# Block transposes that write pairs at a step of 2 elements in place of runs at a step of 4, and loads in two transfers per piece

## The chip, the cores and the metric

The kernel runs on one core of one Trainium2 chip. The metric is the time of one execution on the device in microseconds (us). Engines: VectorE (DVE in the profile), TensorE (PE), ScalarE (ACT), SyncE (SP, which issues the loads here), and the DMA engines.

## The reference

A 1x1 grouped convolution in bf16: every pixel has 192 channels in 4 groups of 48, and each group is multiplied by its own 48x48 matrix.

```python
H = W = 512;  G = 4;  Cg = 48;  C = 192;  k = 1       # x: (1, 512, 512, 192) bf16, w: (1, 1, 4, 48, 48) bf16
xg  = x.reshape(B, H, W, G, Cg)
out = einsum('bhwgc,gcd->bhwgd', xg, w[0, 0]).reshape(B, H, W, C)
```

That is 262,144 pixels, 100.7 MB read and 100.7 MB written.

## The kernel before

Pixels lie on partitions when they are loaded, but the matmuls of this kernel contract over partitions, so the channels must get there. VectorE does this with 32x32 block transposes. One step takes 8 pixel columns (1024 pixels): per partition 4 pixel slots `u` with 384 contiguous elements each, 1536 in all. A transpose instruction (STREAM_TRANSPOSE in the profile) reads these runs in order and writes each 32-element row of a block into `xT`. A column of 128 elements in `xT` is then the stationary operand of a matmul, and the order of the elements in it is the order of the pixels in the matmul's output.

```python
NXT = 4; STEP = 8; NQ = 4; Q = 32; RCOLS = 512        # ring: 512 pixel columns, pieces of at most 128
# [... sizes, planning of pieces: 8, 8, 16, 32, 64, then 128s, then 64, 32, 16, 8, 8 columns ...]

@block.sync                                           # loads, one transfer per piece
def _(sp):
    for p in pieces:
        # [... wait for the stores of the pieces that held this part of the ring ...]
        src = pixels(xf, p).rearrange("(p i) c -> p (i c)", p=128)
        sp.dma_start(region(p), src).then_inc(ld_sem[p.i], 16)

@block.vector                                         # transposes, 256 of them
def _(dve):
    for s in range(NS):
        if s in first:
            wq.wait(ld_sem[first[s].i], 16)
        wq.wait(mm_done, s - NXT + 1)
        src = columns(s).rearrange("p u g (b j) -> p u (g b) j", j=Q)
        dst = xT[s % NXT][:].rearrange("p (b i u) -> p u b i", u=NQ, i=Q)   # i steps 4 elements = 8 bytes
        dve.transpose(dst, src).then_inc(t_done, 1)

# [... tensor: per step 12 matmuls of xT columns with block-diagonal weights, into PSUM ...]
# [... scalar: per step one copy PSUM -> ring, then the store of a finished piece: ...]
        dst = pixels(of, p).rearrange("(a q g) c -> q a (g c)", a=NQ, q=128)
        act.dma_start(dst, region(p).rearrange("p (a n) -> p a n", a=NQ)).then_inc(st_sem[p.i], 16)
```

## Time and profile before

| | before |
|---|---|
| time, median | 897.24 us (3 runs, 897.05 to 898.37) |
| VectorE busy | 874.9 us, 98% of the span of 895.0 us |
| VectorE busy per transpose | 874.9 / 256 = 3.418 us |
| ScalarE, TensorE busy | 371.2 us, 445.0 us |
| DMA | 27.2% + 27.0% of the 16 engines' span |

These are lines of the page of the kernel before: busy time of each engine, the chain of waits that ended last, and the costliest groups of instructions. A group's line gives busy us and the mean ns of one record, then the idle time before it and what ended that.

```profile
PE 445.0 (50%) x3072; PEld 290.0 (32%) x3072; DVE 874.9 (98%) x256; ACT 371.2 (41%) x261; POOL 1.9 (0%) x6
...
DVE 92%; issue 3%; ACTq 2%; PE 1%; DVEq 1%; ACT 0%; DMA 0%
...
L138 DVE STREAM_TRANSPOSE xT<-ring 128x1536 bf16<-128x1536 bf16 x256 | 874.9, 3635 | 14.0 <-PE o_ps L160 10.2
...
L190 ACT CAST ring<-o_ps 128x1536 bf16<-128x1536 f32 x256 | 367.9, 1438 | 510.7 <-PE o_ps L160 488.7
```

VectorE is the bound. One record is 3635 ns, but records of neighbours overlap by some 0.2 us; busy time divided by the count, 3.418 us, is what a step really takes. The timeline of ScalarE in the head of the kernel before (start, duration, engine and line, instructions, and in brackets the idle time before):

```profile
37.49 1.44 ACT L190 CAST ring<-o_ps 128x1536 bf16<-128x1536 f32 x1 [1.98 <-PE o_ps L160]
37.50 23.44 ACTq L184 DMA_DIRECT2D out_dram<-ring  x1
60.98 2.78 ACT L190 CAST ring<-o_ps 128x1536 bf16<-128x1536 f32 x2 [22.05 <-issue]
```

### The profile page before, as it was taken

The numbers are of one execution on the slowest core, as the hardware profiler recorded it, in microseconds if no ns is written. First come the engines' busy times: TensorE is split into PE (matmuls) and PEld (weight loads), VectorE is DVE, ScalarE is ACT, GpSimd is POOL, SyncE is SP. The second block draws the span as 40 slices with busy tenths as digits, with TensorE's granted clock in tenths as the row PEclk, the third lists the DMA queues.
The fourth block names the chain that finished last, engine by engine and source line by source line (L and its number), as shares of the span: only waits on it lengthen the run. The fifth ranks groups of instructions, "written<-read, shape, count | busy, mean of one in ns | idle before, by whom it ended". The sixth has DMA issues, their size and how long they took to land.

```text
span 895.0 us, 7034 instructions
## 1 busy us (share of the span) xinstructions
PE 445.0 (50%) x3072; PEld 290.0 (32%) x3072; DVE 874.9 (98%) x256; ACT 371.2 (41%) x261; POOL 1.9 (0%) x6
## 2 busy tenths in 40 slices
PE   3626766587666544444444434444444444444443
PEld 2314434344443323222232323232232323232222
DVE  8959999999999999999999999999999999999997
ACT  3315344434344344444434344444444343444443
POOL 0000000000000000000000000000000000000000
PEclk9658576755667899999999999999999999999999
DMA  9996419266390844809457192662917633060444
GB/s 385 427 413 252 211 71 388 106 282 282 141 385 38 351 212 192 362 10 389 174 236 327 53 396 114 282 282 97 396 70 299 264 149 133 1 281 1 192 186 185
DMA packets 16413, 201.79 MB, mean 225 GB/s; under 512 B 1024, under 2 KB 4096, under 8 KB 6912
## 3 DMA queue, kind: packets, MB, share of 16 engines
q1 hardware_dynamic: 3456, 100.66, 27.2%
q10 hardware_dynamic: 12928, 100.68, 27.0%
q8 instruction: 25, 0.41, 0.2%
q14 instruction: 4, 0.03, 0.0%
HBM read 100.68 MB, written 100.66 MB: 225 GB/s over the span
## 4 chain that ended last, share of the span: by engine, by line
DVE 92%; issue 3%; ACTq 2%; PE 1%; DVEq 1%; ACT 0%; DMA 0%
DVE xT L138 92%; ACTq L184 2%; PE o_ps L160 1%; DVEq L90 1%; ACT ring L190 0%; DMA ring<-in_x_dram 0%
## 5 line engine op out<-in xcount | busy, mean ns | idle before, releaser
L138 DVE STREAM_TRANSPOSE xT<-ring 128x1536 bf16<-128x1536 bf16 x256 | 874.9, 3635 | 14.0 <-PE o_ps L160 10.2
L160 PE MATMUL o_ps<-wt,xT 128*128 128x192 bf16 (+1 forms) x3072 | 445.0, 303 | 445.4 <-DVE xT L138 412.2
L190 ACT CAST ring<-o_ps 128x1536 bf16<-128x1536 f32 x256 | 367.9, 1438 | 510.7 <-PE o_ps L160 488.7
L160 PEld LDWEIGHTS o_ps<-wt,xT 128*128 128x128 bf16 x3072 | 290.0, 107 | 600.2 <-DVE xT L138 474.8
L176 ACT ACT_TABLE_LOAD x1 | 1.3, 1283 | 9.8 <-DMA w_sb<-in_w_dram 9.8
L176 ACT COPY wt<-w_sb 32x384 bf16<-32x384 bf16 x4 | 2.0, 510 | 0.1
L117 POOL MEMSET wt<- 128x1536 bf16 x1 | 1.4, 1372 | 0.0
L116 POOL MEMSET w_sb<- 32x384 bf16 x1 | 0.4, 407 | 0.3 <-POOLq L212 0.3
L212 POOL MEMSET const-bfloat16-1.0<- 128x1 bf16 x1 | 0.1, 102 | 0.0
L212 POOL MEMSET const-uint8-127<- 128x1 uint8 x1 | 0.1, 102 | 0.0
L212 POOL MEMSET const-float32-0.0<- 128x1 f32 x1 | 0.1, 99 | 0.2 <-issue 0.2
L212 POOL MEMSET const-float32-1.0<- 128x1 f32 x1 | 0.1, 99 | 0.0
## 6 DMA issues: line engine op xcount, KB each, us to landing
ring<-in_x_dram SPq DMA_DIRECT2D x14, 6144.0 KB, 18.0
out_dram<-ring ACTq DMA_DIRECT2D x14, 6144.0 KB, 16.5
ring<-in_x_dram SPq DMA_DIRECT2D x2, 3072.0 KB, 13.5
out_dram<-ring ACTq DMA_DIRECT2D x2, 3072.0 KB, 9.9
ring<-in_x_dram SPq DMA_DIRECT2D x2, 1536.0 KB, 11.8
out_dram<-ring ACTq DMA_DIRECT2D x2, 1536.0 KB, 19.7
ring<-in_x_dram SPq DMA_DIRECT2D x4, 384.0 KB, 9.8
ring<-in_x_dram SPq DMA_DIRECT2D x2, 768.0 KB, 10.9
```

The source lines that it names most:

```text
L90: with ExitStack() as es:
L116: gp.memset(w_sb[:], 0.0).then_inc(wz_sem, 1)
L117: gp.memset(wt[:], 0.0).then_inc(tz_sem, 1)
L138: dve.transpose(dst, src).then_inc(t_done, 1)
L160: ins = pe.matmul(o, lhsT=xs[:, at:at + 128], rhs=r, start=(b == 1), stop=(b == 2), skip_group_check=True)
L176: act.copy(dst, w_sb[:]).then_inc(wc_sem, 1)
L184: act.dma_start(dst, src).then_inc(st_sem[p.i], 16)
L190: act.copy(dst, src).then_inc(o_done, 1)
L212: nc = _bacc.Bacc("TRN2", target_bir_lowering=False, num_devices=1)
```

## The change

The intent: let consecutive writes of a transpose land close together, in pairs of neighbouring 4-byte words, while the loads keep packets half as long as before. Writes of one run go to elements 0, 2, then 8, 10, then 16, 18 and so on, in place of 0, 4, 8, 12. To make the pixel order come out right, a piece is loaded as two transfers, each with a packet of 24,576 bytes per partition for the large pieces, not 49,152.

```diff
-                src = pixels(xf, p).rearrange("(p i) c -> p (i c)", p=128)
-                sp.dma_start(region(p), src).then_inc(ld_sem[p.i], 16)
+                src = pixels(xf, p).rearrange("(r u b n) c -> u r b (n c)", r=64, u=2, b=2)
+                half = p.size * C // 2
+                for u in range(2):
+                    sp.dma_start(region(p)[:, u * half:(u + 1) * half], src[u]).then_inc(ld_sem[p.i], 16)
 ...
-                    wq.wait(ld_sem[first[s].i], 16)
+                    wq.wait(ld_sem[first[s].i], 32)
                 wq.wait(mm_done, s - NXT + 1)
-                src = columns(s).rearrange("p u g (b j) -> p u (g b) j", j=Q)
-                dst = xT[s % NXT][:].rearrange("p (b i u) -> p u b i", u=NQ, i=Q)
+                src = columns(s).rearrange("p (w v) g n -> p w v (g n)", w=2, v=2)
+                dst = xT[s % NXT][:].rearrange("p (b w i v) -> p w v b i", w=2, i=2, v=2)
                 dve.transpose(dst, src).then_inc(t_done, 1)
```

## The prediction

Passages that say of the hardware what no trace or run of this case shows are cut from the prediction and from the expectations, and the cuts are marked. In the prediction the two terms of the step are a cost per element and a fixed cost per instruction, neither taken from a trace; their sum was a pitch of 1.69 to 1.82 us. The sums that follow rest on it: 433 to 466 us over 256 steps, 239 x 1.7 to 1.8 us on the VectorE path and, coupled with DMA, the forecast of 508 us.

> **What bounds the kernel now.** VectorE. The page's first part has it busy 874.9 of 895.0 us (98%), and the chain of waits is 92% the block transpose. In the stage-by-stage chain sixteen transposes (one 128-column piece) take 54.66 us, so the pitch is 3.416 us, for 1536 elements per partition: 2.22 ns an element. 256 x 3.416 = 874.5 us. Everything else has room: ScalarE's eviction 1.44 us a step (368 us in all); TensorE's 12 matmuls 1.48 us a step at full clock (2.74 us at the low clock of the first 300 us); DMA busy 27.2 + 27.0% of the span, 487 us.
>
> **Why the transpose costs 2.2 ns.** Source runs are contiguous; writes step 4 elements (8 bytes)[...].[...]
>
> **What the change does.** Same instruction count on VectorE, TensorE, ScalarE. Write order becomes element 0, 2, then 8, 10, then 16, 18: pairs in adjacent words[...]. Expected: [...]1.69 to 1.82 us pitch[...], 433 to 466 us over 256 steps, about 420 us saved, all on the critical path. Loads go from 24 to 48 transfers, their packets from 49,152 to 24,576 bytes; the records show 1.815 us and 0.912 us for those sizes, the same rate, so no DMA cost. Smaller load packets should let stores, which share the DMA engines with them, through sooner.
>
> **What binds next.** DMA. Packets at 0.912 us (loads) and 0.465 us (12,288-byte stores) sum to 472 us; the stretches where DMA was saturated moved 406 to 429 GB/s, so 201.3 MB take 470 to 495 us. Some 15 to 25 us are lost early: the four ring slots are filled by about 60 us and the next load waits for stores, and ScalarE sat 23.4 us in issuing the fourth store[...]. That stall should shrink. VectorE path: about 55 to 62 us of head (17 steps done), 239 x 1.7 to 1.8 = 406 to 430, tail 8: 470 to 500 us. DMA path: about 490 to 510. They are close and coupled by the ring, so I add a little: 508 us.
>
> **Chances.** Faster 0.87; within 2% 0.10 (2-byte writes don't merge[...]); slower 0.03.
>
> **What would show it.** Transpose record about 1.9 us (3.635 before; records overlap by 0.22), pitch under 1.85; VectorE busy 435 to 470 us; DMA share over 90% in most slices; the chain of waits split between VectorE and DMA/ScalarE issue; TensorE clock near full after the start[...]; matmul and eviction durations unchanged; load landing times longer, since loads now contend with stores.
>
> **What would make it wrong.** The transpose stays near 3.4 us (no merging of half-word writes, or the transposer itself needs two cycles an element): 897 us. Partial merging, 2.3 to 2.8 us pitch: 640 to 760 us. TensorE stuck at low clock (2.74 us a step): about 720 us. ScalarE blocking repeatedly in store issues because DMA is saturated (up to 20 us for each of 14 large stores): 560 to 650 us. Ring too shallow for mixed loads and stores: 520 to 560 us.

## More of the kernel before

The only stop of VectorE that is worth looking at is 10.2 us on TensorE.

ScalarE's sequencer stood 23.44 us in the issue of its fourth store. No PSUM was emptied in that time, so TensorE stopped (19.4 us on ScalarE, its longest such wait), then VectorE (10.2 us on TensorE).

## The result, and the profile after

| | before | after |
|---|---|---|
| time, median | 897.23 us (4 runs) | 887.22 us (4 runs, 886.95 to 887.44) |
| ratio | | 0.9886, 95% interval 0.9869 to 0.9903 |
| VectorE busy | 874.9 us | 874.4 us |
| VectorE busy per transpose | 3.418 us | 3.416 us |
| VectorE idle before transposes | 14.0 us | 4.6 us |

The gain is clear of the noise (the interval excludes 1), but it is 1.1%, not the 43% that the prediction's 508 us would have been. Ratios in this document are the mean time of one kernel's fast runs over that of the other's of the same rounds, so they are not quite the ratio of the medians beside them.

The same lines of the page after the change:

```profile
PE 382.2 (43%) x3072; PEld 257.4 (29%) x3072; DVE 874.4 (99%) x256; ACT 371.8 (42%) x261; POOL 1.9 (0%) x6
...
DVE 95%; issue 4%; DVEq 1%; DMA 0%; PE 0%; ACT 0%; SPq 0%
...
L140 DVE STREAM_TRANSPOSE xT<-ring 128x1536 bf16<-128x1536 bf16 x256 | 874.4, 3617 | 4.6 <-DMA ring<-in_x_dram 4.6
```

The transpose did not get faster at all: 874.4 us busy for the same 256 instructions. VectorE still bounds the kernel. What the change won, 10 us, is the stop of 10.2 us on TensorE, which is gone. ScalarE's timeline in the head after the change:

```profile
37.04 1.44 ACT L192 CAST ring<-o_ps 128x1536 bf16<-128x1536 f32 x1 [1.97 <-PE o_ps L162]
37.05 5.43 ACTq L186 DMA_DIRECT2D out_dram<-ring  x1
42.52 2.79 ACT L192 CAST ring<-o_ps 128x1536 bf16<-128x1536 f32 x2 [4.04 <-issue]
```

The same store issue now holds ScalarE for 5.43 us, short enough for the buffers between the engines to hide it: all of the 4.6 us that VectorE still stood idle went to a load. In the books of the profiles: 10.2 us of stop less, 0.5 us less of busy time, 0.9 us more of waiting for the first load (4.6 against 3.7 us in the two lists of waits); the span fell by 9.8 us.

So there were two questions. Is the 10 us really the work of the two transfers? And why did the new write order do nothing?

### The profile page after: what moved, and what is told of

Same layout as the page of the kernel before. It is cut to its first block, busy times and chain, and to the rows that moved or that the text cites. A ratio compares the mean times of both kernels' runs of the same rounds, so it can differ in the third digit from the quotient of the medians.

```text
span 885.2 us, 7058 instructions
## 1 busy us (share of the span) xinstructions
PE 382.2 (43%) x3072; PEld 257.4 (29%) x3072; DVE 874.4 (99%) x256; ACT 371.8 (42%) x261; POOL 1.9 (0%) x6
## 4 chain that ended last, share of the span: by engine, by line
DVE 95%; issue 4%; DVEq 1%; DMA 0%; PE 0%; ACT 0%; SPq 0%
DVE xT L140 95%; DVEq L90 1%; DMA ring<-in_x_dram 0%; PE o_ps L162 0%; ACT ring L192 0%; SPq L129 0%
## 5 line engine op out<-in xcount | busy, mean ns | idle before, releaser
L140 DVE STREAM_TRANSPOSE xT<-ring 128x1536 bf16<-128x1536 bf16 x256 | 874.4, 3617 | 4.6 <-DMA ring<-in_x_dram 4.6
L162 PE MATMUL o_ps<-wt,xT 128*128 128x192 bf16 (+1 forms) x3072 | 382.2, 275 | 498.4 <-DVE xT L140 488.6
L162 PEld LDWEIGHTS o_ps<-wt,xT 128*128 128x128 bf16 x3072 | 257.4, 98 | 622.9 <-DVE xT L140 545.8
## 6 DMA issues: line engine op xcount, KB each, us to landing
ring<-in_x_dram SPq DMA_DIRECT2D x28, 3072.0 KB, 17.4
```

Of the source, the lines that this page charges most:

```text
L162: ins = pe.matmul(o, lhsT=xs[:, at:at + 128], rhs=r, start=(b == 1), stop=(b == 2), skip_group_check=True)
```

## The experiments

In all of them the comparison is the kernel before, run on the same chip. "Busy per step" is the VectorE busy time of the page over 256; the recorded texts call the time from step to step the pitch. A cycle in the expectations: no run measured one; read it as about the time of an element in step1, 1.08 ns. "Write port" and "transposer" there are names for what VectorE does in writing and in transposing; no run shows these parts by themselves. Sixteen kernels ran. Ten gave wrong results: they write the same number of bytes into `xT` in an order that the rest of the kernel does not expect, so times hold and results do not.

### split_only: two transfers, old write order

```diff
-                sp.dma_start(region(p), src).then_inc(ld_sem[p.i], 16)
+                half = p.size * C // 2
+                for u in range(2):
+                    sp.dma_start(region(p)[:, u * half:(u + 1) * half], src[:, u * half:(u + 1) * half]).then_inc(ld_sem[p.i], 16)
...
-                    wq.wait(ld_sem[first[s].i], 16)
+                    wq.wait(ld_sem[first[s].i], 32)
```

> The change's two transfers per piece, with the old write order (step 4). Theory (the 10 us came from the head: smaller load packets let the first store drain sooner, so ScalarE's fourth store issue blocks for about 5 us in place of 23 and VectorE does not stop for TensorE): 887 us, ratio 0.989, transpose pitch 3.416 us. Rival (the gain comes from the new write order or pixel order): 897 us, and the 10.2 us stop of VectorE stays.

Measured: correct, 886.47 us median (4 runs) against 896.97 us, ratio 0.9882 (0.9865 to 0.9898). First the group of transposes on its page, then the store issue in ScalarE's timeline:

```profile
L140 DVE STREAM_TRANSPOSE xT<-ring 128x1536 bf16<-128x1536 bf16 x256 | 875.1, 3607 | 3.8 <-DMA ring<-in_x_dram 3.8
```

```profile
36.40 7.12 ACTq L186 DMA_DIRECT2D out_dram<-ring  x1
```

The whole gain of the change is there without its write order and its pixel order. The issue blocks for 7.12 us, more than the 5 us expected, and VectorE no longer stops. This run also had a mean granted TensorE clock of 0.62, against 1.0 in the profile after the change, and the same time: TensorE's clock did not matter here, with VectorE at 3.4 us a step.

Why do shorter packets help? Loads and stores share the 16 DMA engines: in the kernel before, the load queue had exactly 16 packets in flight at once for 206 us of the span, and the store queue for 201 us. The trace does not name the engine of a packet record, so how an engine takes turns between them is not shown. What the traces show is that the first store waits longer beside longer loads. It is 512 packet records of 768 bytes. From its first to its last packet it took 40.2 us before, beside loads of up to 49,152 bytes (1.815 us each), 26.2 us after, beside loads of up to 24,576 bytes (0.912 us each), and 8.9 us in run2 below, where the large loads have 12,288 bytes (0.460 us each).

The blocked fourth issue follows this first store. It ended 1.5 us before the store's last packet in the kernel before (60.94 and 62.44 us), 2.4 us before it after the change (42.48 and 44.89 us) and 2.5 us before it here; in run2 the first store was through before the fourth issue, which took 0.38 us. That the issue waits until most of the first store is through is an inference from these times; no run took it apart further. The number of load transfers changed together with the length of their packets in all these runs, so the gain of the two transfers is shown, and the length of the packets as its reason is argued.

### step1: adjacent writes

```diff
-                dst = xT[s % NXT][:].rearrange("p (b i u) -> p u b i", u=NQ, i=Q)
+                dst = xT[s % NXT][:].rearrange("p (b u i) -> p u b i", u=NQ, i=Q)
```

> Wrong result on purpose (pixels land in another order): before with transposes that write runs of 32 adjacent elements, nothing else changed. Theory A (the transposer itself takes about two cycles per element, so the write pattern is hidden behind it): record 3.6 us, pitch 3.416 us, 895 to 897 us. Theory B (2-byte writes do not merge in pairs of 4-byte words at step 2, but adjacent ones do): pitch 1.7 to 1.85 us and 480 to 560 us.

Measured: wrong result, 497.81 us.

```profile
PE 380.5 (77%) x3072; PEld 258.8 (52%) x3072; DVE 425.8 (86%) x256; ACT 369.8 (75%) x261; POOL 1.9 (0%) x6
...
L138 DVE STREAM_TRANSPOSE xT<-ring 128x1536 bf16<-128x1536 bf16 x256 | 425.8, 1734 | 42.9 <-PE o_ps L160 35.4
```

Busy per step is 1.663 us. Theory A, a transposer that needs two cycles an element, has fallen: only the write order was altered, and the time per element fell from 2.22 to 1.08 ns. The write order is what makes the transpose slow.

### halves: two transposes of half the size

```diff
-                dve.transpose(dst, src).then_inc(t_done, 1)
+                dve.transpose(dst[:, 0:2], src[:, 0:2])
+                dve.transpose(dst[:, 2:4], src[:, 2:4]).then_inc(t_done, 1)
```

> Before with each transpose cut into two of 768 elements. It measures slope and fixed cost of one transpose. Theory A (a cost per element of about 2 cycles): [...]a step takes 3.45 to 3.65 us and the run 905 to 960 us. Rival C (a large part of the 3.4 us is a fixed cost per instruction, such as a flush): a step takes clearly longer, 4.5 us or more, over 1150 us.

Measured: correct, 896.95 us.

```profile
PE 385.5 (43%) x3072; PEld 260.0 (29%) x3072; DVE 874.9 (98%) x512; ACT 371.2 (41%) x261; POOL 1.9 (0%) x6
```

VectorE was busy 874.9 us with 512 instructions, the same as with 256. There is no fixed cost to be seen in this write order, where theory A expected a step of 3.45 us or more (the terms of its sum were an assumption): the 3.4 us are entirely a cost per element.

### wide: lone writes 96 bytes apart

```diff
-                dst = xT[s % NXT][:].rearrange("p (b i u) -> p u b i", u=NQ, i=Q)
+                dst = xT[s % NXT][:].rearrange("p (i u b) -> p u b i", u=NQ, i=Q)
```

> Wrong result on purpose: before with each write 48 elements (96 bytes) from the one before. Theory A: if the write port needs less than the transposer's two cycles per element even here, pitch stays 3.416 us and 897 us[...]. Theory B (the write pattern sets the cost): pitch clearly over 3.416 us[...].

Measured: wrong result, 1869.14 us.

```profile
L138 DVE STREAM_TRANSPOSE xT<-ring 128x1536 bf16<-128x1536 bf16 x256 | 1856.2, 7639 | 3.8 <-DMA ring<-in_x_dram 3.8
```

Busy per step is 7.251 us, or 4.72 ns an element. The write order alone more than doubled the time, which theory B expected and theory A did not.

### run2, run4, run8: adjacent elements, then a hop

These are correct kernels. To have 2, 4 or 8 adjacent elements, the pixel order needs four transfers per piece, with packets of 12,288 bytes. With n = 2, 4, 8:

```diff
-                src = pixels(xf, p).rearrange("(p i) c -> p (i c)", p=128)
-                sp.dma_start(region(p), src).then_inc(ld_sem[p.i], 16)
+                src = pixels(xf, p).rearrange("(r u b n) c -> u r b (n c)", r=128 // n, u=NQ, b=n)
+                part = p.size * C // NQ
+                for u in range(NQ):
+                    sp.dma_start(region(p)[:, u * part:(u + 1) * part], src[u]).then_inc(ld_sem[p.i], 16)
...
+                    wq.wait(ld_sem[first[s].i], 64)
...
+                src = columns(s).rearrange("p u g n -> p u (g n)")
+                dst = xT[s % NXT][:].rearrange("p (b u i) -> p u b i", u=NQ, i=n)
```

> Correct kernel: each transpose writes two adjacent elements (one whole 4-byte word), then hops 16 bytes; pieces load in four transfers of 12,288-byte packets. Theory W (a write costs about 2.2 ns whatever fills it, and two adjacent 2-byte elements share one write of a 4-byte word; the change left every write a half-filled word): pitch 1.66 to 1.75 us, 480 to 510 us, bound by DMA. Theory G (a whole 8-byte unit, four adjacent elements, must be filled): pitch 2.5 to 3.4 us, 650 to 897 us. Theory L (only long runs are fast): pitch about 3.4 us, 887 us.

> As run2 with runs of four adjacent elements (8 bytes). Theory W: as run2. Theory G: 1.66 to 1.75 us pitch and 480 to 510 us here, but not in run2. Theory L: still about 3.4 us or in between.

> As run2 with runs of eight adjacent elements (16 bytes). Theory W and G: 1.66 us pitch and 480 to 510 us. Theory L: slower than that. If run2, run4 and run8 share a pitch, their times show whether the load order (how many DRAM rows lie beside each other) matters to DMA: expected within 1% of each other.

| | median | ratio to before | busy per step |
|---|---|---|---|
| run2 | 489.38 us | 0.545 (0.5441 to 0.546) | 426.8 / 256 = 1.667 us |
| run4 | 489.52 us | 0.545 (0.5442 to 0.5458) | 426.8 / 256 = 1.667 us |
| run8 | 546.24 us | 0.6085 (0.606 to 0.6111) | 427.2 / 256 = 1.669 us |

Two adjacent elements in each 16-byte hop are enough; theories G and L have fallen. The transposes of all three cost the same, and run2 and run4 beat both kernels. The page of run2 shows what binds now; its lines are the busy times, the DMA share of the span in 40 slices, the GB/s in the same slices, the two large queues, and the transposes:

```profile
PE 394.2 (81%) x3072; PEld 271.0 (56%) x3072; DVE 426.8 (88%) x256; ACT 369.8 (76%) x261; POOL 1.9 (0%) x6
...
DMA  6999999999999999999999999999999999999998
GB/s 173 378 423 428 424 425 426 427 432 426 428 433 426 428 432 428 427 432 428 426 434 428 426 433 428 425 432 428 426 431 428 426 434 427 421 428 373 379 411 294
...
q1 hardware_dynamic: 13824, 100.67, 49.6%
q10 hardware_dynamic: 12928, 100.68, 49.2%
...
L140 DVE STREAM_TRANSPOSE xT<-ring 128x1536 bf16<-128x1536 bf16 x256 | 426.8, 1757 | 49.0 <-DMA ring<-in_x_dram 49.0
```

The two queues fill 98.8% of the DMA engines' time, and VectorE's idle time is all waiting for loads. With one core running and half of the bytes read and half written, most slices show 421 to 434 GB/s.

run8 missed its expectation of 1%. Its transposes are as fast, but VectorE waited 106.3 us for loads:

```profile
L140 DVE STREAM_TRANSPOSE xT<-ring 128x1536 bf16<-128x1536 bf16 x256 | 427.2, 1748 | 106.3 <-DMA ring<-in_x_dram 106.3
```

Its load packets of 12,288 bytes, 460 ns in run2 and run4, had a median of 582 ns over the first 200 us of the span. In the loads, only the order in which a transfer visits the partitions and the DRAM differs from run4. Why this slows the packets was not followed up and stays open.

### step2_long: uniform step of 2

```diff
-                src = columns(s).rearrange("p u g (b j) -> p u (g b) j", j=Q)
-                dst = xT[s % NXT][:].rearrange("p (b i u) -> p u b i", u=NQ, i=Q)
+                src = columns(s).rearrange("p (w v) g n -> p w v (g n)", w=2, v=2)
+                dst = xT[s % NXT][:].rearrange("p (b w i v) -> p w v b i", w=2, i=Q, v=2)
```

> Wrong result on purpose: one load per piece as before, writes at a uniform step of 2 elements over runs of 32, so that there is no hop of 16 bytes after each pair. Theory W: each write still half fills a word, pitch 3.416 us, 897 us. Rival (step 2 would have been fast, but the hop after every pair spoiled it): pitch 1.66 to 1.9 us, about 500 us.

Measured: wrong result, 501.91 us.

```profile
L138 DVE STREAM_TRANSPOSE xT<-ring 128x1536 bf16<-128x1536 bf16 x256 | 446.5, 1838 | 40.1 <-PE o_ps L160 34.9
```

Busy per step is 1.744 us. My theory W fell here: every write half fills a word, and the order is fast all the same. A step of 2 is good; what the change did with it, two writes and then a hop, is not. A new theory had to explain four write orders at once. Counting how many writes fall into one 16-byte line before the order moves on does it (call it theory N): 1 in wide, 2 before, 2 after the change, 4 in step2_long, and each such visit costs about 4.5 ns. Orders with an innermost step of 1 are outside it. That is a fit; the next four runs test it.

### quad2: the change with runs of four

```diff
-                src = pixels(xf, p).rearrange("(r u b n) c -> u r b (n c)", r=64, u=2, b=2)
+                src = pixels(xf, p).rearrange("(r u b n) c -> u r b (n c)", r=32, u=2, b=4)
...
-                dst = xT[s % NXT][:].rearrange("p (b w i v) -> p w v b i", w=2, i=2, v=2)
+                dst = xT[s % NXT][:].rearrange("p (b w i v) -> p w v b i", w=2, i=4, v=2)
```

The diff is against the changed kernel: elements 0, 2, 4, 6, then 16, 18, 20, 22.

> Correct kernel, one number of the change altered: runs of four elements at step 2 (four half-filled words, one whole 16-byte line), then a hop of 32 bytes; two transfers per piece as in the change. Theory N (half-filled writes are paid by the 16-byte line visited, about 4.3 cycles each, whatever number of them falls in the line; fits before, the change, step2_long and wide): 4 writes per line, pitch 1.73 to 1.76 us as in step2_long, 485 to 500 us. Rival H (any hop spoils step 2, only long uniform runs are fast): pitch 2.5 to 3.4 us, 650 to 887 us.

Measured: correct, 497.0 us median (4 runs, 495.72 to 497.75) against 897.4 us, ratio 0.5533 (0.552 to 0.5547).

```profile
L140 DVE STREAM_TRANSPOSE xT<-ring 128x1536 bf16<-128x1536 bf16 x256 | 432.9, 1825 | 49.1 <-DMA ring<-in_x_dram 27.2
```

Busy per step is 1.691 us, a little less than expected. A hop after each run does no harm if the run has four writes in its line. This is the change as it was meant: two transfers, packets of 24,576 bytes, and 400 us gained. Its fourth store issue still blocks, for 16.55 us, and 21.9 us of VectorE's idle time are stops on TensorE; run2, whose fourth issue does not block, is 7.6 us faster. The mean distance between writes is 8 bytes an element, as before and as in the change, so the mean distance cannot be what costs (1.691 us a step here against 3.418 and 3.416 us).

### step3 and step8: the slope

```diff
 step3
-                src = columns(s).rearrange("p u g (b j) -> p u (g b) j", j=Q)
-                dst = xT[s % NXT][:].rearrange("p (b i u) -> p u b i", u=NQ, i=Q)
+                src = columns(s).rearrange("p u g n -> p u (g n)").rearrange("p u (t j) -> p u t j", t=3)
+                dst = xT[s % NXT][:].rearrange("p (u j t) -> p u t j", u=NQ, t=3)
 step8
+                src = columns(s).rearrange("p u g (b j) -> p u (g b) j", j=Q).rearrange("p u (c t) j -> p u c t j", t=2)
+                dst = xT[s % NXT][:].rearrange("p (c i t u) -> p u c t i", u=NQ, i=Q, t=2)
```

> Wrong result on purpose: before with single writes at a step of 3 elements, 2.67 writes per 16-byte line on average. Theory N: 4.3 / 2.67 = 1.6 cycles an element, pitch 2.5 to 2.7 us, 660 to 710 us. Rival (an 8-byte unit is what counts, 1.33 writes in each at about 2.1 cycles): also 1.6 cycles; but that rival has quad2 no different from step2_long and the change fast, so it is only a check of the slope. A step function (anything but a step of 2 is slow): pitch 3.4 us.

> Wrong result on purpose: before with single writes at a step of 8 elements, one half-filled word in each 16-byte line, lines next to each other. Theory N: 4.3 to 4.5 cycles an element, pitch 6.8 to 7.25 us as in wide, 1760 to 1870 us. Rival D (the cost of a lone write grows with the distance, and 16 bytes is near): pitch 3.4 to 5 us, 890 to 1300 us.

Measured, wrong results: step3 692.82 us, step8 1756.06 us. The transposes of step3, then those of step8:

```profile
L138 DVE STREAM_TRANSPOSE xT<-ring 128x1536 bf16<-128x1536 bf16 x256 | 657.7, 2700 | 27.2 <-PE o_ps L160 22.8
```

```profile
L138 DVE STREAM_TRANSPOSE xT<-ring 128x1536 bf16<-128x1536 bf16 x256 | 1743.1, 7196 | 3.8 <-DMA ring<-in_x_dram 3.8
```

Busy per step is 2.569 us and 6.809 us, both inside what theory N expected, the second just so (the run of step8 is 4 us under its range). Neighbouring lines cost nearly as much as lines 96 bytes apart (4.43 ns an element against 4.72 ns in wide), so rival D has fallen.

### pair_far: adjacent pairs 192 bytes apart

```diff
-                src = columns(s).rearrange("p u g (b j) -> p u (g b) j", j=Q)
-                dst = xT[s % NXT][:].rearrange("p (b i u) -> p u b i", u=NQ, i=Q)
+                src = columns(s).rearrange("p u g (b h i) -> p u (g b) h i", h=Q // 2, i=2)
+                dst = xT[s % NXT][:].rearrange("p (h u b i) -> p u b h i", u=NQ, h=Q // 2, i=2)
```

> Wrong result on purpose: before with two adjacent elements per write (one whole word), then a hop of 192 bytes. If whole words escape the cost of a line[...]: pitch 1.66 us, about 497 us. If every line visited costs about 4.3 cycles at long hops also for whole words: pitch 3.4 to 3.6 us, 890 to 940 us.

Measured: wrong result, 498.07 us.

```profile
L138 DVE STREAM_TRANSPOSE xT<-ring 128x1536 bf16<-128x1536 bf16 x256 | 425.7, 1738 | 43.0 <-PE o_ps L160 35.8
```

Busy per step is 1.663 us. Two adjacent elements, one whole 4-byte word, pay nothing visible for a new line, at hops of 16 bytes (run2, 1.667 us) and of 192 bytes (here): step1, without hops, has 1.663 us too.

### word_adj and word_lone: 4-byte elements

Is it the whole word that escapes, or the innermost step of 1? Here pairs of elements move as one 4-byte element, 768 per step, adjacent in the control and 16 bytes apart in the other.

```diff
+                src = columns(s).rearrange("p u g n -> p u (g n)").bitcast(F32).rearrange("p u (b j) -> p u b j", j=Q)
 word_adj
+                dst = xT[s % NXT][:].bitcast(F32).rearrange("p (b u i) -> p u b i", u=NQ, i=Q)
 word_lone
+                dst = xT[s % NXT][:].bitcast(F32).rearrange("p (b i u) -> p u b i", u=NQ, i=Q)
```

> Wrong result on purpose (pairs of elements move as one 4-byte element): control for word_lone, 768 elements of 4 bytes per partition written in runs of 32 adjacent words. Both theories: about one element per cycle, a record near 0.8 to 1.0 us and a run bound by DMA, 485 to 500 us; if the transposer moves two bytes a cycle, 1.66 us.

> Wrong result on purpose: as word_adj, but one whole 4-byte word per 16-byte line, step 16 bytes, no innermost step of 1. Theory N (only writes that half fill a word pay for the line): the record is that of word_adj within 15%. Rival S (the instruction is fast when its innermost step is 1, and lone writes pay for the line whatever they fill): 768 x 4.4 ns = 3.4 us.

Measured, wrong results: 496.41 and 494.17 us, both bound elsewhere, so the record of one transpose is what counts. First word_adj, then word_lone:

```profile
L138 DVE STREAM_TRANSPOSE xT<-ring 128x768 f32<-128x768 f32 x256 | 247.9, 975 | 214.1 <-PE o_ps L160 165.4
```

```profile
L138 DVE STREAM_TRANSPOSE xT<-ring 128x768 f32<-128x768 f32 x256 | 382.6, 1565 | 78.2 <-PE o_ps L160 37.8
```

word_adj met its expectation; for word_lone neither theory held. Lone whole words are not free (1565 ns against 975, 60% more, where theory N allowed 15%), and they do not cost 4.4 ns either: busy per step over 768 words is 1.95 ns a word. So at a step of 16 bytes a lone write costs 1.95 ns if it fills a word and 4.43 ns if it fills half of one (step8). It would also explain pair_far, if two adjacent elements are written as one word: they take 2.17 ns to stream, which covers one whole-word write. No run shows that they are.

### copy_step8 and copy_step4: the same patterns without a transpose

```diff
-                dve.transpose(dst, src).then_inc(t_done, 1)
+                dve.tensor_copy(dst, src).then_inc(t_done, 1)
```

This line alone is altered, in step8 and in before.

> Wrong result on purpose: step8 with a plain copy in place of the transpose, same access patterns. If the cost of about 4.4 ns per half-filled line belongs to the write port, the copy takes 3.4 us[...] to 6.8 us. If it belongs to the transposer, [...]about 490 to 500 us.

> Wrong result on purpose: before with a plain copy in place of the transpose. Write port: half of copy_step8 (two writes per line), 1.7 to 3.4 us. Transposer: [...]about 490 to 500 us.

Measured, wrong results: 897.25 and 499.86 us. First copy_step8, then copy_step4:

```profile
L138 DVE COPY xT<-ring 128x1536 bf16<-128x1536 bf16 x256 | 874.9, 3928 | 14.2 <-PE o_ps L160 10.4
```

```profile
L138 DVE COPY xT<-ring 128x1536 bf16<-128x1536 bf16 x256 | 441.9, 1999 | 39.6 <-PE o_ps L160 34.4
```

Busy per step is 3.418 and 1.726 us, half of what the transposes of the same patterns take (6.809 and 3.418), and again a factor of two between one and two writes per line. Per line visited that is 2.23 and 2.25 ns, where the transposes have 4.43 and 4.45 ns. The cost belongs to VectorE's writes, not to the transposer: copy_step8 took 3.418 us, where a transposer's cost, by estimate, would have left about the 1.66 us of step1 or less. copy_step4 alone would not have told the two apart. Why a copy pays half of what a transpose pays for a line is not shown.

### The line count in one table

Half-filled words only; all figures are busy per step / 1536 elements; the last two rows are the copies.

| kernel | writes per 16-byte line visit | ns per element | ns per line visit |
|---|---|---|---|
| wide | 1 | 4.72 | 4.72 |
| step8 | 1 | 4.43 | 4.43 |
| before | 2 | 2.22 | 4.45 |
| after the change | 2 | 2.22 | 4.45 |
| step3 | 2.67 on average | 1.67 | 4.46 |
| step2_long | 4 | 1.14 | 4.54 |
| quad2 | 4 | 1.10 | 4.40 |
| copy_step8 | 1 | 2.23 | 2.23 |
| copy_step4 | 2 | 1.12 | 2.25 |

Adjacent elements (step1, run2) stream at 1.08 ns each, so four half-filled writes per line come within 5% of that rate (1.10 and 1.14 ns), and two take twice as long (2.22 ns). The copies pay half for a line, but by the same count. No other size of line fits these rows: the change and step2_long both put two writes into each 8 bytes, the change and quad2 both put four into each 32 bytes, and yet the change takes twice as long per element as either. What happens inside the memory was not measured; the runs show the count, not the mechanism. Why wide is 6% above step8 is open.

## Why the prediction was wrong, point by point

- **VectorE bounds the kernel; the step takes 3.416 us.** Right, and still so after the change.
- **"Why the transpose costs 2.2 ns."** The reason given there, for which no trace was the source, put a cost on each lone write, and I took the measured 2.22 ns an element, which fell into its band, for agreement. This agreement carried no weight. One number inside a wide band does not tell two mechanisms apart: two half-filled writes to a line at 4.45 ns give the same 2.2 ns. That it fell into the band was luck. The fixed cost per instruction that I took off first was not there either (halves: 874.9 us for 256 transposes as for 512).
- **"1.69 to 1.82 us pitch".** This is the step that failed. I assumed that a pair of writes to neighbouring words is enough for the fast pitch; half-filled words need four in a 16-byte line (1.691 us in quad2). The change kept two per line, as before, so its pitch is 3.416 us, as before. The gain of 420 us was never started; nothing took it back later. quad2, with four per line, has 1.691 us, the pitch that the change was expected to have.
- **"2-byte writes don't merge", 0.10.** Close to the reason for the miss, and with far too small a chance: step2_long and quad2 (1.14 and 1.10 ns an element) show that half-filled writes do share the cost of a line, but the pairs of the change shared it no better than the writes before (2.22 ns both). The other listed reason, a transposer that needs two cycles, was shown wrong by step1.
- **DMA binds next, "about 490 to 510".** Right, though not in this change, which never got there; it is shown by the kernels whose transposes are fast: 489.4 (run2), 497.0 (quad2), 497.8 us (step1), with the DMA engines at 90% or more in 38, 36 and 34 of the 40 slices. Loads landed later with the DMA engines this full, as expected: from issue to landing the large ones took, in the median, 27.6 us in quad2 against 17.4 us after the change, and 24.2 us in step1 against 18.0 us before.
- **"no DMA cost" for halved packets, and "That stall should shrink".** Right: a packet took 1.815 us for 49,152 bytes and 0.912 us for 24,576, and the issue fell from 23.44 to 5.43 us and VectorE's stop vanished. I had counted it as a minor term; it is the whole of the measured 10 us, as split_only shows.
- **TensorE's clock.** I listed a stuck clock as a risk. It was between 0.62 and 1.0 in runs of equal time (886.83 us in split_only, 886.95 us after the change), and played no part.

## What to carry to other kernels

When VectorE writes 2-byte elements with a step, count how many consecutive writes fall into one 16-byte line before the order leaves it: in these transposes each line visited cost 4.4 to 4.7 ns, in the copies 2.2 to 2.3 ns, whatever the mean step, so that fewer than four writes per line were slow (3.418 us a step with two, 1.691 us with four in quad2), and two adjacent elements escaped altogether (1.667 us in run2). A cost that was measured with one element size is a guess for another (a lone write at a step of 16 bytes took 1.95 ns with 4-byte elements, 4.43 ns with 2-byte ones), and agreement of one number with a band is not a test; a kernel that differs in one access pattern tells in one run what the pattern costs. A gain that appears beside the one that was meant (10 us, from loads in two transfers) should be taken apart by running half of the change.
